# Sink-window attention and SoLU layer on one core: the first chunk's loads issued from ScalarE, and w_in's blocks fetched and split first

## The chip, the cores and the metric

One core of a Trainium2 chip runs the whole kernel. The metric is device time in microseconds (us), the median of a few runs. A profile of one execution of the kernel before is at hand; all its times count from the start of its span.

Short names: PE is the matmul engine TensorE (PEld its weight load), DVE is VectorE, ACT is ScalarE, POOL is GpSimd, SP is SyncE, whose queue issues DMAs. "Row" means a line of a view of the profile; L441 is line 441 of the kernel.

## The reference

```python
def _attn_ref(q, k, v, n_sink, window):          # 4 batches, 8 heads, 768 tokens, 64 per head
    scores = scale * np.matmul(q, k.transpose(0, 1, 3, 2))
    keep = is_sink | in_window                   # key < n_sink, or 0 <= query - key < window
    scores = np.where(keep, scores, -1000000000.0)
    a = np.exp(scores - np.max(scores, axis=-1, keepdims=True))
    a = a / (np.sum(a, axis=-1, keepdims=True) + 1e-09)
    return np.matmul(a, v)

def _moe_ref(x, w_in, w_out, g_ln):              # x: 3072 x 512, w_in: 512 x 1024, w_out: 1024 x 512
    h = x @ w_in
    e = np.exp(h - np.max(h, axis=-1, keepdims=True))
    solu = h * e / (np.sum(e, axis=-1, keepdims=True) + 1e-09)
    ln = (solu - mean) / np.sqrt(var + 1e-06) * g_ln
    return ln @ w_out
```

The drawn scalars are n_sink = 4 and window = 128. The two weights, the gain g_ln and the scalars come as 64-bit numbers; q, k and v as 32-bit floats.

## The kernel before

The 3,072 tokens are cut into 24 chunks of 128, numbered `n`, two batches in turn. A chunk passes some fifty stages: loads of k, q and v (`load_k`, `load_q`, `load_v`, all through `load`), transposes of q and k on PE (`turn`, L526), copies on ACT (`kf`, `qf`), scores per head (L604 for chunks 0 and 1, L606 and L607 for the others), the masked minimum on DVE (L624), exponentials on ACT (L634), normalisation on POOL, transposes of the weights `ptp`, the product with v (`av`, `xp`), then `h` = x·w_in (L772), the SoLU and layer norm, the transposes `utp`, `o` = u·w_out (L841), and the store.

The products with the two weights are done in three passes, with every operand split into a high and a low part. The splitting of the weights is done on the chip, in 16 blocks of 512 KB: blocks 0 to 7 are w_in (`w1h`, `w1l`), 8 to 15 are w_out (`w2h`, `w2l`). A block j passes these stages:

- `fetch_w`, a DMA into `wraw_j`;
- `lower_w` on ACT (L411), then `move_w`, `sign_w` and `rest_w` on DVE (L415, L419, L424), which make `wbits_j` from the 64-bit words;
- `sum_w`, a matmul into the PSUM tile `ws_j` (L441); for w_in there is one such tile at a time (`ps_h` has one buffer);
- `w_hi` on ACT (L449, for w_out L451 with the gain), `less_w` on PE (L455), `w_lo` on ACT (L459), which frees `ws_j`.

Three small loads stand beside them (`fetch_small`): the two scalars into `words`, the gain into `g_rows`, and the first rows of v. `words` passes a few POOL operations, a matmul (`spread_0`) and an ACT copy (`val`) before POOL can make the masks, `bias0` first; `g_rows` passes `spread_1` and the copy `g_sb`.

Nothing reorders this work at run time. Each stage of each chunk and block has a number, a due time, in the tables `PLAN`, `PLAN_W`, `FIRST` and `OWN` (the last for chunks 0 to 3, 22 and 23). All steps are sorted by it, and each engine's program gets its instructions in that order and runs them in that order; an instruction whose input is late holds all behind it on its engine. DMA issues are instructions of the queue's engine in the same sense.

The built program gives each DMA from SP's and ACT's queues one of eight completion semaphores (DMAHW0 to DMAHW7), in turn over both queues in the order of the sorted steps. A DMA that gets a semaphore for the second time is issued only when the DMA that had it before has landed; on which queue that one was does not matter.

Of the kernel before, what the change touches and what calls it, by code (L numbers as in the profile page):

```python
# [11 lines left out]
I32 = mybir.dt.int32  # L12
# [19 lines left out]
    "score": (-33.44, -29.74, -32.95, -26.95, -28.22, -30.8, -25.49, -21.19),  # L32
# [5 lines left out]
    "turn_p": (-17.35, -13.82),  # L38
# [34 lines left out]
    "round_ident": (-3163.34,),  # L73
    "gains": (-344.53, -1257.3, -494.63, -210.32, 7.7, -70.04, -35.97, -251.92, -3187.03),
    "outside": (181.94,),
    "fetch_small": (-3957.07, -334.9, -3898.57),
    "scalars": (-1567.28,),
    "spread": (-1567.18, -1257.7),
    "take_small": (-1567.08, -1257.5),
    "masks": (-1279.21, -432.35, -165.0),  # L80
    "fetch_w": (-405.15, -3960.38, -426.29, -3880.5, -3919.36, -3952.13, -3953.56, -417.09, -3892.48, -3917.91,
                -3984.79, -352.47, -151.19, -383.05, -132.13, -412.11),
    "lower_w": (-322.59, -1511.91, -340.85, -464.5, -1518.94, -3256.59, -3271.05, -342.81, -551.25, -1488.73,
                -3298.13, -259.68, -126.59, -247.18, -65.79, -329.82),
    "move_w": (-278.19, -1291.02, -319.05, -426.7, -1268.02, -2053.29, -2135.99, -342.63, -474.7, -1311.88, -2065.14,
               -242.49, -126.04, -206.92, -64.64, -318.86),
    "sign_w": (-159.49, -1266.75, -280.91, -419.12, -514.59, -2051.66, -2009.32, -327.68, -447.58, -1267.77,
               -2054.73, -219.39, -79.66, -139.64, -54.37, -316.39),
    "rest_w": (-155.59, -517.15, -155.98, -388.61, -341.51, -2042.38, -1259.65, -242.66, -366.45, -1238.15, -521.74,
               -206.56, -69.38, -91.58, -32.25, -243.78),  # L90
    "sum_w": (-119.83, -422.04, -96.33, -336.21, -229.53, -1475.65, -702.46, -156.13, -302.03, -648.8, -436.66,
              -80.12, 29.82, -32.53, 15.53, -217.15),
    "w_hi": (-128.31, -479.01, -100.46, -341.71, -328.13, -1468.88, -984.48, -230.1, -337.05, -577.13, -482.82,
             -120.05, -19.66, -38.33, -27.91, -142.74),
    "less_w": (-118.42, -381.66, -88.15, -328.34, -206.16, -1389.51, -691.27, -137.84, -264.23, -448.45, -338.06,
               -54.35, 33.19, -26.02, 16.19, -99.77),
    "w_lo": (-100.5, -348.23, -79.88, -324.36, -159.61, -1257.51, -570.51, -129.19, -260.8, -350.76, -260.82, -44.19,
             33.91, -21.12, 20.58, -87.29),
# [74 lines left out]
P = 128  # L173
# [56 lines left out]
def _banded(ctx, tc, q, k, v, n_sink, window, w_in, w_out, g_ln, out, val, wts, wpool, consts):  # L230
    nc = tc.nc
# [8 lines left out]
    KT2 = DFF // P  # L240
# [37 lines left out]
    def fetch_small(_, j):  # L278
        if j == 0:
            for i, s in enumerate((n_sink, window)):  # L280
                nc.sync.dma_start(words[0:1, i, :], s.bitcast(I32).rearrange("(o w) -> o w", o=1))
# [192 lines left out]
    def load(n, nm, src, bufs):  # L474
        b, c = place(n)
# [566 lines left out]
```

## Time and profile before

| what | value |
|---|---|
| median of 3 runs | 497.99 us (497.97 to 498.84) |
| the profiled execution | 498.57 us |
| its span | 496.9 us, 9093 instructions |
| PE busy | 468.7 us, 94% of the span |
| PEld, DVE, ACT, POOL busy | 388.4, 390.5, 354.4, 316.1 us |
| DMA, over the span | 51.78 MB, mean 104 GB/s |
| DMA, 12.4 us slices, the first four | 275, 307, 196, 171 GB/s |

The profiled execution lies 0.58 us above the median. PE is the busiest engine, but a share of the whole span says little about a change at its beginning: the stretches of the first 60 us have to be read one by one, and in them each engine's first rows with the idle time ahead of each and what ended it.

### The profile page before, as it was taken

To read this page: it belongs to the slowest core of one execution; us is meant where nothing else is said; L and a number is where in the kernel's file an instruction comes from. 1 tells how busy PE (TensorE), PEld (TensorE's weight loads), DVE (VectorE), ACT (ScalarE), POOL (GpSimd) and SP (SyncE) were. 2 spreads that over 40 slices of the span, in tenths; PEclk is the share of its full clock that TensorE was granted. 3 is DMA by queue.
4 is the path that set the end of the run, shared out by engine and by line. 5 is a ranking of instruction groups with operands and counts; after the bars stand their busy time and mean duration, and the time that the engine had idled before them with its cause. 6 is when DMAs were issued, how large, how long until landed. Compare 5 with 4: busy or idle time off the path is not lost.

```text
span 496.9 us, 9093 instructions
## 1 busy us (share of the span) xinstructions
PE 468.7 (94%) x2631; PEld 388.4 (78%) x2631; DVE 390.5 (79%) x1195; ACT 354.4 (71%) x957; POOL 316.1 (64%) x439
## 2 busy tenths in 40 slices
PE   0989999999899999999999999999999999999995
PEld 0444767888788888888888888888888888887873
DVE  2878999899987588798799988888888879766631
ACT  4798997787785667776876786676777787675352
POOL 3675576588666557678646386676776776667610
PEclk9978999999999999999999999999999999999999
DMA  8966154354265353522555363464264262201101
GB/s 275 307 196 171 43 108 106 85 122 113 61 140 119 75 117 84 120 67 54 119 136 106 79 139 68 113 138 107 53 141 106 54 144 61 57 28 44 44 22 47
DMA packets 101099, 51.78 MB, mean 104 GB/s; under 512 B 78956, under 2 KB 90228, under 8 KB 101044
## 3 DMA queue, kind: packets, MB, share of 16 engines
q1 hardware_dynamic: 101044, 51.14, 42.4%
q8 instruction: 23, 0.38, 0.3%
q14 instruction: 32, 0.26, 0.2%
HBM read 27.53 MB, written 6.42 MB: 68 GB/s over the span
## 4 chain that ended last, share of the span: by engine, by line
PE 73%; DVE 9%; ACT 5%; POOL 5%; issue 4%; DMA 2%; SPq 0%; DVEq 0%; POOLq 0%
PE o L841 22%; PE h L772 21%; PE s L606 4%; PE s L607 4%; PE utp L826 4%; PE av L721 3%; PE ptp L652 3%; PE av L724 3%; PE ws L441 2%; PE kt L526 2%; PE qt L526 2%; PE av L726 1%; DVE y L734 1%; DVE ring L579 1%; DMA wraw<-in_moe_w_in_dram 1%
## 5 line engine op out<-in xcount | busy, mean ns | idle before, releaser
L841 PE MATMUL o<-w2h,uh 128*128 128x512 f32 x192 | 79.2, 412 | 0.0
L772 PE MATMUL h<-w1h,xh 128*128 128x512 f32 x192 | 77.5, 403 | 0.6 <-DVE u L794 0.6
L634 ACT ACTIVATE sc<-sc,nmx 128x136 f32<-128x136 f32 (+1 forms) x192 | 76.4, 402 | 1.7 <-DVE nmx L624 1.2
L772 PE MATMUL h<-w1l,xh 128*128 128x512 f32 x192 | 75.9, 395 | 0.0
L841 PE MATMUL o<-w2h,ul 128*128 128x512 f32 x192 | 75.7, 394 | 0.0
L734 DVE TENSOR_REDUCE y<-av 128x256 f32<-128x512 f32 x88 | 60.3, 687 | 19.5 <-PE av L726 17.0
L772 PE MATMUL h<-w1h,xl 128*128 128x512 f32 x192 | 75.7, 394 | 0.0
L841 PE MATMUL o<-w2l,uh 128*128 128x512 f32 x192 | 75.6, 394 | 0.0
L669 POOL TENSOR_SCALAR_AFFINE_SELECT pc<-pt 128x1024 fp32r<-128x1024 f32 x40 | 43.8, 1095 | 33.3 <-DVE pt L662 17.0
L624 DVE CUSTOM_DVE_ANT_0 sc<-s,bias 128x136 f32<-128x136 f32 (+1 forms) x192 | 54.4, 295 | 10.1 <-PE s L604 2.9
L645 POOL TENSOR_TENSOR sc<-sc,rs 128x544 f32<-128x544 f32 (+1 forms) x48 | 52.2, 1089 | 15.5 <-DVE rs L640 8.7
L606 PE MATMUL s<-ring,qT 128*128 128x264 f32 (+1 forms) x176 | 56.2, 321 | 2.6 <-DVE nmx L624 1.4
L761 POOL TENSOR_TENSOR xl<-xt,xh 128x256 fp32r<-128x256 f32 x44 | 32.4, 737 | 28.9 <-ACT xh L756 22.5
L607 PE MATMUL s<-ring,qX 128*128 128x264 f32 (+1 forms) x176 | 49.7, 285 | 0.3 <-DMA qX<-qT 0.3
L721 PE MATMUL av<-pc,vs 128*128 128x256 f32 x160 | 44.3, 299 | 1.3 <-ACT ob L846 0.9
L675 POOL TENSOR_SCALAR_AFFINE_SELECT pt<-pt 128x1024 fp32r<-128x1024 f32 x40 | 43.6, 1091 | 1.6
L830 ACT CAST uh<-utp 128x512 fp32r<-128x512 f32 x48 | 28.0, 586 | 21.3 <-PE utp L826 21.1
L834 DVE TENSOR_TENSOR ul<-utp,uh 128x512 fp32r<-128x512 f32 x48 | 33.0, 687 | 12.8 <-ACT uh L830 12.1
L772 PEld LDWEIGHTS h<-w1h,xl 128*128 128x128 f32 x192 | 36.1, 188 | 8.9
L841 PEld LDWEIGHTS o<-w2h,ul 128*128 128x128 f32 x192 | 36.1, 188 | 8.7 <-DVE ul L834 0.2
L606 PEld LDWEIGHTS s<-ring,qT 128*128 128x128 f32 x176 | 33.1, 188 | 11.9 <-issue 3.6
L574 ACT CAST ring<-kt 64x512 fp32r<-64x512 f32 x44 | 25.4, 578 | 22.9 <-DVE ring L579 21.8
(147 smaller groups left out, 1300.7 us busy)
## 6 DMA issues: line engine op xcount, KB each, us to landing
qX<-qT SPq DMA_DIRECT2D x88, 128.0 KB, 2.2
kn<-in_k_dram SPq DMA_DIRECT2D x24, 256.0 KB, 3.5
qn<-in_q_dram SPq DMA_DIRECT2D x24, 256.0 KB, 4.1
vn<-in_v_dram SPq DMA_DIRECT2D x24, 256.0 KB, 4.3
out_dram<-ob SPq DMA_DIRECT2D x24, 256.0 KB, 3.5
ysh<-y SPq DMA_DIRECT2D x88, 64.0 KB, 2.0
wraw<-in_moe_w_out_dram SPq DMA_DIRECT2D x8, 512.0 KB, 4.0
wraw<-in_moe_w_in_dram SPq DMA_DIRECT2D x8, 512.0 KB, 6.6
```

Source lines behind the costliest of these rows:

```text
L606: nc.tensor.matmul(o, st["qT", n, x][:, r, :], rhs, start=True, stop=False)
L607: nc.tensor.matmul(o, st["qX", n, x][:, r, :], rhs, start=False, stop=True)
L624: nc.vector.tensor_tensor_reduce(out=st["sc", n, hb][:, j, c0:c1], in0=st["s", n, h].rearrange("p a x -> p (a x)")[:, c0:c1], in1=bias0 if ...
L634: nc.scalar.activation(sc[:, i, c0:c1], sc[:, i, c0:c1], AF.Exp, bias=nmx[:, i:i + 1], scale=-1.0, accum_out=ssum[:, i:i + 1])
L645: nc.gpsimd.tensor_tensor(sc[:, :, c0:c1], sc[:, :, c0:c1], rs.unsqueeze(2).to_broadcast([P, HB, c1 - c0]), op=ALU.mult)
L669: nc.gpsimd.affine_select(pc, pt.bitcast(F32), pattern=[[0, HB * 2], [1, P]], compare_op=ALU.is_ge, fill=0.0, base=0, channel_multiplier=-1)
L675: nc.gpsimd.affine_select(pt, pt.bitcast(F32), pattern=[[0, HB * 2], [-1, P]], compare_op=ALU.is_ge, fill=0.0, base=-1, channel_multiplier=1)
L721: nc.tensor.matmul(acc[:, x], lhs, pc[:, 2 * jp + x], start=(x == 0), stop=(alone and x == 1))
L734: nc.vector.tensor_reduce(st["y", n, hb][:, jp], st["acc", n, pr].rearrange("p x s q -> p x q s"), axis=AX.X, op=ALU.add)
L772: nc.tensor.matmul(st["h", n][:, cols], a[:, kt % 2, :], w[:, kt, cols], start=(kt == 0 and m == 0), stop=(kt == KT1 - 1 and m == 2))
L834: nc.vector.tensor_tensor(ul, st["utp", n, g4], st["uh", n, g4].bitcast(F32), op=ALU.subtract)
L841: nc.tensor.matmul(st["o", n], a[:, kt % 4, :], part(w, kt), start=(kt == 0 and m == 0), stop=(kt == KT2 - 1 and m == 2))
```

## The change

Three things are changed.

- Five DMAs go from SP's queue to ACT's: the loads of chunk 0's keys and queries (`kn_0`, `qn_0`), the two scalars, and the gain.
- The due times of the weight blocks and of chunks 0 to 3, 22 and 23 are other numbers. The blocks of w_in are fetched ahead of most of w_out's, and block 5 of w_in is the first on SP's queue and the first that DVE makes.
- Two entries of `PLAN` move by 0.09 and 0.25: one score (head 5) and the second transpose of the weights `ptp`. They hold for all chunks without numbers of their own.

```diff
 PLAN = {
-    "score": (-33.44, -29.74, -32.95, -26.95, -28.22, -30.8, -25.49, -21.19),
+    "score": (-33.44, -29.74, -32.95, -26.95, -28.22, -30.71, -25.49, -21.19),
...
-    "turn_p": (-17.35, -13.82),
+    "turn_p": (-17.35, -13.57),
 PLAN_W = {
-    "fetch_small": (-3957.07, -334.9, -3898.57),
+    "fetch_small": (-5146.64, -294.06, -5149.48),
...
-    "fetch_w": (-405.15, -3960.38, -426.29, -3880.5, -3919.36, -3952.13, -3953.56, -417.09, -3892.48, -3917.91,
+    "fetch_w": (-5089.45, -5149.5, -5086.99, -5118.34, -5146.5, -5149.71, -5148.45, -418.64, -5103.25, -5146.01,
...
 def fetch_small(_, j):
-                nc.sync.dma_start(words[0:1, i, :], s.bitcast(I32).rearrange("(o w) -> o w", o=1))
+                nc.scalar.dma_start(words[0:1, i, :], s.bitcast(I32).rearrange("(o w) -> o w", o=1))
...
-            nc.sync.dma_start(g_rows[0:KT2], g_ln.rearrange("(kt p) -> kt p", p=P))
+            nc.scalar.dma_start(g_rows[0:KT2], g_ln.rearrange("(kt p) -> kt p", p=P))
 def load(n, nm, src, bufs):
-        nc.sync.dma_start(t, src[b, :, c * P:(c + 1) * P, :].rearrange("h p d -> p h d"))
+
+        (nc.scalar if n == 0 and nm != "vn" else nc.sync).dma_start(
+            t, src[b, :, c * P:(c + 1) * P, :].rearrange("h p d -> p h d"))
```

What the new numbers do is shown by the order of the instructions. Lines of the changed kernel lie one to three higher than those of the kernel before (L411 is L412, L526 is L529). A name such as `wraw_10_125` is the tile `wraw` of block 10; the last number only counts tiles. What stands behind "waits" are the semaphores that the instruction waits for.

ACT's first rows before: the table load, then blocks 10, 6 and 5, then the constants and the scalars' copy, blocks 4, 1 and 9, and the first `w1h`.

```order
L411 ACT_TABLE_LOAD
L411 ACTIVATE wbits_10_148<-wraw_10_125 128x512 [waits DMAHW0_49]
L411 ACTIVATE wbits_6_150<-wraw_6_131 128x512 [waits DMAHW4_49]
L411 ACTIVATE wbits_5_152<-wraw_5_133 128x512 [waits DMAHW5_49]
L434 ACTIVATE dg_8_154<-ident_89 128x128 [waits Pool_49]
L262 CAST ident_r_94<-ident_89 128x128
L309 COPY val_58<-spread_0_169 128x2 [waits PE_49]
L411 ACTIVATE wbits_4_172<-wraw_4_135 128x512 [waits DMAHW6_49]
L411 ACTIVATE wbits_1_174<-wraw_1_127 128x512 [waits DMAHW1_49]
L411 ACTIVATE wbits_9_176<-wraw_9_137 128x512 [waits DMAHW7_49]
L449 CAST w1h_62<-wbits_5_152 128x512 [waits DVE_49]
```

The same place on ACT now.

```order
L287 DMA g_rows_99<-in_moe_g_ln_dram 8x128 [waits Pool_49]
L282 DMA words_95<-in_n_sink_dram 1x2
L282 DMA words_95<-in_window_dram 1x2 [waits DMAHW0_49]
L479 DMA kn_0_140<-in_k_dram 128x8x64 [waits DMAHW1_49]
L412 ACT_TABLE_LOAD
L412 ACTIVATE wbits_1_142<-wraw_1_127 128x512
L435 ACTIVATE dg_8_144<-ident_89 128x128
L479 DMA qn_0_146<-in_q_dram 128x8x64 [waits DMAHW4_49]
L412 ACTIVATE wbits_5_158<-wraw_5_125 128x512
L263 CAST ident_r_94<-ident_89 128x128
L412 ACTIVATE wbits_6_161<-wraw_6_130 128x512 [waits DMAHW2_49]
L412 ACTIVATE wbits_4_163<-wraw_4_136 128x512
```

Five DMAs moved into ACT's program, four ahead of the table load and `qn_0` ahead of block 5's `lower_w`. DMAHW0, 1 and 4 were given before to `wraw_5`, `wraw_1` and `wraw_4`, the first, second and fifth blocks on SP's queue (next fences).

SP's first rows before.

```order
L402 DMA wraw_10_125<-in_moe_w_out_dram 128x1024
L402 DMA wraw_1_127<-in_moe_w_in_dram 128x1024
L281 DMA words_95<-in_n_sink_dram 1x2
L281 DMA words_95<-in_window_dram 1x2
L402 DMA wraw_6_131<-in_moe_w_in_dram 128x1024
L402 DMA wraw_5_133<-in_moe_w_in_dram 128x1024
L402 DMA wraw_4_135<-in_moe_w_in_dram 128x1024
L402 DMA wraw_9_137<-in_moe_w_out_dram 128x1024
L477 DMA kn_0_139<-in_k_dram 128x8x64
L477 DMA qn_0_141<-in_q_dram 128x8x64
L286 DMA g_rows_99<-in_moe_g_ln_dram 8x128
```

SP's first rows now.

```order
L403 DMA wraw_5_125<-in_moe_w_in_dram 128x1024
L403 DMA wraw_1_127<-in_moe_w_in_dram 128x1024
L403 DMA wraw_6_130<-in_moe_w_in_dram 128x1024
L403 DMA wraw_10_132<-in_moe_w_out_dram 128x1024
L403 DMA wraw_4_136<-in_moe_w_in_dram 128x1024
L403 DMA wraw_9_138<-in_moe_w_out_dram 128x1024
L403 DMA wraw_3_148<-in_moe_w_in_dram 128x1024
L403 DMA wraw_8_150<-in_moe_w_out_dram 128x1024
L403 DMA wraw_0_152<-in_moe_w_in_dram 128x1024
L403 DMA wraw_2_154<-in_moe_w_in_dram 128x1024
L479 DMA qn_1_156<-in_q_dram 128x8x64
L403 DMA wraw_15_247<-in_moe_w_out_dram 128x1024
```

Ten weight blocks now stand in a row; `kn_1` follows `wraw_15`, where before it stood ahead of it.

PE's first rows now; before, `spread_1` stood behind `kt_0`, the queries' transposes ahead of the keys', and `ws_9`'s first matmul between the scores 6 and 5.

```order
L305 MATMUL spread_1_176<-ident_89,g_rows_99 128x128
L303 MATMUL spread_0_178<-alone_98,ones_f_100 128x2
L442 MATMUL ws_5_186<-wbits_5_158,dg_8_144 128x512
L456 MATMUL ws_5_186<-w1h_62,ident_r_94 128x512
L529 MATMUL kt_0_189<-ident_89,kn_0_140 128x128 x4
L529 MATMUL qt_0_194<-ident_89,qn_0_146 128x128 x4
L442 MATMUL ws_6_224<-wbits_6_161,dg_8_144 128x512
L456 MATMUL ws_6_224<-w1h_62,ident_r_94 128x512
L607 MATMUL s_0_3_227<-kf_0_219,qf_0_222 128x128
L607 MATMUL s_0_6_229<-kf_0_219,qf_0_222 128x128
L607 MATMUL s_0_5_240<-kf_0_219,qf_0_222 128x128
L607 MATMUL s_0_4_242<-kf_0_219,qf_0_222 128x128
```

The same eight groups of matmuls as before lead up to the first score `s_0_3`; behind it the scores 6, 5 and 4 follow at once, and `ws_9` has moved behind them.

More of the change, by code (lines that the diff above doesn't have):

```diff
@@ L72 @@
 PLAN_W = {
-    "round_ident": (-3163.34,),
-    "gains": (-344.53, -1257.3, -494.63, -210.32, 7.7, -70.04, -35.97, -251.92, -3187.03),
-    "outside": (181.94,),
-    "fetch_small": (-3957.07, -334.9, -3898.57),
[L77 to L80, printed above, removed]
-    "fetch_w": (-405.15, -3960.38, -426.29, -3880.5, -3919.36, -3952.13, -3953.56, -417.09, -3892.48, -3917.91,
-                -3984.79, -352.47, -151.19, -383.05, -132.13, -412.11),
@@ L83 @@
[L83 to L98, printed above, removed]
+    "round_ident": (-3361.62,),
+    "gains": (-377.83, -1251.67, -437.6, -147.52, 15.46, -84.04, -17.22, -232.77, -5129.02),
+    "outside": (150.82,),
+    "fetch_small": (-5146.64, -294.06, -5149.48),
@@ new lines @@
+    "scalars": (-1614.26,),
+    "spread": (-1563.05, -1564.19),
+    "take_small": (-1556.91, -1258.2),
+    "masks": (-1266.51, -449.66, -165.94),
+    "fetch_w": (-5089.45, -5149.5, -5086.99, -5118.34, -5146.5, -5149.71, -5148.45, -418.64, -5103.25, -5146.01,
+                -5146.83, -294.09, -195.78, -295.89, -115.85, -494.09),
+    "lower_w": (-318.67, -5131.58, -316.18, -503.55, -3353.66, -3370.51, -3354.7, -319.11, -490.5, -1526.41,
+                -1536.51, -258.52, -153.06, -233.78, -82.99, -374.2),
@@ new lines @@
+    "move_w": (-298.96, -1396.96, -256.96, -479.95, -2370.06, -2396.73, -2370.87, -258.07, -479.96, -1394.91,
+               -1394.17, -251.39, -133.69, -79.85, -82.35, -342.32),
+    "sign_w": (-258.87, -1396.87, -242.79, -414.94, -1386.81, -2396.45, -2370.15, -255.01, -430.46, -1390.38,
+               -560.71, -168.17, -116.83, -79.43, -50.51, -300.63),
+    "rest_w": (-170.52, -1386.46, -167.25, -414.6, -364.45, -2388.27, -1398.38, -249.55, -419.27, -1384.85, -480.34,
+               -158.9, -83.49, -50.52, -43.69, -299.51),
@@ new lines @@
+    "sum_w": (-137.62, -418.94, -100.45, -313.47, -277.92, -1500.51, -742.35, -195.28, -351.46, -451.41, -382.58,
+              -39.98, 25.81, -14.86, 35.47, -194.66),
+    "w_hi": (-148.39, -488.91, -129.08, -319.86, -316.19, -1541.11, -1267.72, -230.5, -374.6, -484.89, -379.47,
+             -62.35, -51.34, -49.77, -40.8, -131.67),
+    "less_w": (-132.13, -396.99, -92.97, -312.65, -261.04, -1499.03, -699.31, -156.09, -344.7, -441.58, -357.73,
+               -30.75, 28.42, -6.33, 38.21, -103.0),
@@ L99 @@
+    "w_lo": (-110.98, -363.52, -79.97, -280.59, -241.16, -1263.51, -493.14, -148.53, -317.76, -375.78, -329.91,
+             -23.13, 32.49, -5.62, 42.87, -83.4),
 }
```

113 rows, old and new, of the table OWN are left out of this document.

## The prediction

> **What bounds the kernel now.** I read the page first, then the busy times by stretch, and then, since the change sits at the beginning, each engine's first rows in order of time.
>
> ```profile
> span 496.9 us, 9093 instructions
> 0.00:12.50 12.50, 0.58 (x2) 0.50 (x2) 3.33 (x8) 5.09 (x10) 4.31 (x19) 1.00 0.84 275
> 12.50:25.00 12.50, 11.43 (x37) 6.17 (x38) 10.77 (x30) 9.40 (x23) 8.06 (x14) 1.00 1.04 307
> 25.00:40.00 15.00, 12.04 (x41) 6.98 (x40) 11.30 (x31) 13.24 (x30) 9.24 (x12) 0.69 0.60 167
> 40.00:60.00 20.00, 19.14 (x92) 12.17 (x91) 17.34 (x60) 18.73 (x59) 11.55 (x23) 0.98 0.47 121
> 90.00:120.00 30.00, 30.00 (x181) 25.59 (x180) 26.64 (x84) 22.37 (x66) 22.15 (x29) 1.00 0.36 87
> 400.00:480.00 80.00, 79.04 (x437) 66.76 (x437) 55.22 (x157) 49.86 (x128) 50.05 (x66) 1.00 0.22 58
> 480.00:497.00 17.00, 10.70 (x50) 8.06 (x48) 3.27 (x9) 5.39 (x9) 0.81 (x2) 0.94 0.10 35
> ```
>
> The columns after the length are PE, PEld, DVE, ACT and POOL busy, PE's granted clock, the DMA share and GB/s. From 40 us on PE is idle for 0.86 of 20 us, then for almost nothing up to 480 us: it is the bound, and its work is the same after the change. So the time changes by what PE loses or wins before 40 us, where it is idle for 11.92 + 1.07 + 2.96 = 15.95 us, and by a little at the end. Up to 25 us the 16 DMA engines are full (share 0.84, with the start-up in it, and 1.04), so the order in which blocks land decides what can start.
>
> ```profile
> 0.80 1.28 ACT L411 ACT_TABLE_LOAD   x1 [0.80 <-PEq L1024]
> 4.28 0.59 SPq L477 DMA_DIRECT2D kn<-in_k_dram  x1
> 4.29 0.66 ACT L411 ACTIVATE wbits<-wraw 128x512 f32<-128x512 f32 x1 [2.21 <-DMA wraw<-in_moe_w_out_dram]
> 6.12 2.60 SPq L477 DMA_DIRECT2D qn<-in_q_dram  x1
> 8.44 0.66 ACT L411 ACTIVATE wbits<-wraw 128x512 f32<-128x512 f32 x1 [3.49 <-DMA wraw<-in_moe_w_in_dram]
> 8.84 3.24 SPq L286 DMA_DIRECT2D g_rows<-in_moe_g_ln_dram  x1
> 9.74 0.67 ACT L411 ACTIVATE wbits<-wraw 128x512 f32<-128x512 f32 x1 [0.65 <-DMA wraw<-in_moe_w_in_dram]
> 10.54 0.42 DVE L415 TENSOR_SCALAR wbits<-wbits 128x512 int32<-128x512 int32 x1
> 10.98 2.05 ACT L411 ACTIVATE wbits<-wraw 128x512 f32<-128x512 f32 x3
> 11.72 0.69 DVE L424 SCALAR_TENSOR_TENSOR wbits<-wraw,wbits 128x512 int32<-128x512 int32 x1
> 12.55 2.05 PE L441 MATMUL ws<-wbits,dg 128*128 128x512 f32 x2 [4.71 <-DVE wbits L424]
> 12.94 0.60 ACT L449 CAST w1h<-wbits 128x512 fp32r<-128x512 f32 x1
> 13.61 1.42 PE L455 MATMUL ws<-w1h,ident_r 128*128 128x512 f32 x1
> 14.82 1.05 PE L526 MATMUL qt<-ident,qn 128*128 128x128 f32 x4
> 15.06 0.60 ACT L459 ACTIVATE w1l<-ws 128x512 fp32r<-128x512 f32 x1 [1.52 <-PE ws L455]
> 15.84 2.48 DVE L424 SCALAR_TENSOR_TENSOR wbits<-wraw,wbits 128x512 int32<-128x512 int32 x4
> 16.53 0.42 PE L304 MATMUL spread<-ident,g_rows 128*128 128x128 f32 x1
> 16.98 0.17 ACT L311 COPY g_sb<-spread 128x8 f32<-128x8 f32 x1 [1.32 <-PE spread L304]
> 17.52 0.60 ACT L548 COPY qf<-qt 128x512 f32<-128x512 f32 x1
> 18.70 0.50 PE L455 MATMUL ws<-w1h,ident_r 128*128 128x512 f32 x1 [0.75 <-ACT w1h L449]
> 19.12 0.49 PE L604 MATMUL s<-kf,qf 64*128 64x128 f32 x4
> 19.78 0.29 DVE L624 CUSTOM_DVE_ANT_0 sc<-s,bias 128x128 f32<-128x128 f32 x1 [0.76 <-PE s L604]
> ```
>
> Three things are to be seen. The eight semaphores show: `kn_0`, the ninth DMA, is issued at 4.28, when the first block lands (ACT takes it at 4.29), and `qn_0` only at 6.12, so the second block lands then. The blocks land at 4.29, 6.12, at most 8.44, 9.74 and at most 10.98, where ACT takes three lowers without a gap, the fifth block's first. And from ACT's `lower_w` of block 5 at 9.74 to its first matmul at 12.55 there are 2.81 us, which set PE's first real work.
>
> **The change, part by part.** *The DMAs on ACT.* Before, all five cost ACT nothing. Now ACT issues `g_rows` and one scalar, waits for the first block (4.29) to issue the other, waits for the second (6.12) to issue `kn_0` (0.59), and only then loads its table (1.28): 6.12 + 0.59 + 1.28 = 7.99. Block 1's `lower_w` follows to 8.65; before, ACT only had one lower behind it at that time, so that much is hidden. Not hidden is `qn_0`: it waits for the fifth block. That lands between 9.74 (the fourth before) and 10.98, plus up to half a block's spacing of (9.74 - 4.29) / 3 = 1.82, since `kn_0` with half a block's bytes now travels among the first five. I take 11.0, and 0.59 for the issue, as for `kn_0` on SP; at the ends 9.9 and 0.4, or 11.9 and 2.60, `qn_0`'s own row. ACT reaches block 5's lower at 11.6 (10.3 to 14.5), against 9.74.
>
> A rule speaks against this part in any case. The Trainium skill, DMA: Bandwidth & Descriptors, section Issuing engines are not separate DMA queues, says that DMAs from all queues run on the same 16 engines, and that spreading the issue saves only the issuing sequencer's time. The shares of 0.84 and 1.04 above agree that the engines were full already. By it alone the part would be worth nothing.
>
> *Block 5 first on DVE.* DVE's first rows are now all of block 5, so PE's first split starts at 11.6 + 2.81 = 14.4, against 12.55: 1.85 later (0.6 to 4.8). `w1h` follows at 14.4 (12.94 before), `less_w` at 15.0 (13.61).
>
> *The first transposes.* Two sets take 16.53 - 14.82 = 1.71, so they run from 15.4 to 17.1 instead of to 16.53. The queries' come second, at 16.2. `qn_0`, issued at 11.0, lands at 15.1 by the median of its kind, and is in time:
>
> ```profile
> qn<-in_q_dram SPq DMA_DIRECT2D x24, 256.0 KB, 4.1
> 22.42 1.12 PE L441 MATMUL ws<-wbits,dg 128*128 128x512 f32 x2
> ```
>
> `spread_1` is out of the way early, which takes away the 1.32 us ahead of `g_sb`.
>
> *To the first score.* DVE makes block 6 behind block 5: 14.4 + 0.41 + 0.62 + 0.41 + 0.62 = 16.5 (0.62 is 2.48 / 4; 0.41 and 0.62 likewise for L415 and L419). Then on ACT `w1h` of block 6, `w1l` of block 5, `g_sb`, `kf`, a ring cast and `qf` at 0.5 to 0.6 each: 19.6. The first score starts at 19.6 instead of 19.12. DVE has 12 instructions between block 5 and the first masked minimum, 4 x 0.41 + 8 x 0.62 = 6.6: 21.0 instead of 19.78, with block 10 two instructions (1.24) less far than before. The scores that now follow at once have only two PSUM buffers and wait for these minima; `ws_9`, which filled that time before, stands behind them.
>
> ```profile
> 28.68 0.48 PE L604 MATMUL s<-kf,qf 64*128 64x128 f32 x2 [1.18 <-ACT kf L570]
> 29.71 0.49 PE L604 MATMUL s<-kf,qf 64*128 64x128 f32 x2
> 30.00:42.50 12.50, 10.87 (x35) 6.14 (x34) 9.65 (x25) 10.97 (x27) 5.16 (x9) 0.59 0.39 90
> DMA to landing us min/median/max: 4.8/6.6/9.2
> ```
>
> *To chunk 1's scores.* The minima let the scores 5, 4 and 7 go by 22.4; then come block 9 (1.12 + 0.50, the rows of L441 above and of L455), `qt_1` (0.86), block 1 (1.62), block 10 (1.12) and three scores: `kt_1` at about 28, its copy `kf` done at 29.5, the first score of chunk 1 at about 30, against 29.71. So most is caught up, since `qt_1` now comes early and DVE had idle time. But at that point PE lacks both matmuls of block 3 (1.62), with one of block 8 (1.12) as the offset, 0.5 + 0.3 = 0.8 in all, and ACT lacks two lowers and a `w1h` (2 x 0.67 + 0.60), less a ring cast (0.6), 1.3. I take 1.1, between the two. `kn_1`, which now waits behind `wraw_15` for DVE's block 9 (21.0), lands 4.8 us later (the last line above, for the loads of k in the first 60 us), at 25.8, and is not needed before 27.
>
> *The middle and the end.* In chunks 4 to 21 the new numbers swap one transpose group with one score or with the `utp` beside it; in chunks 22 and 23 groups change places, but the same work stands behind the last `h`.
>
> ```profile
> PE s L606 <- DVE nmx L624: 1.1, 3, 0.7
> PE av L721 <- ACT ob L846: 0.9, 2, 0.7
> ```
>
> These are PE's longest waits from 60 us on (total, times, longest). One such wait more or less is 0.7 us; I take 0 for both, and 0.7 either way for the range.
>
> *Sum.* +1.1 in the head, 0 behind it. The profiled execution's 498.57 becomes 499.7. It stands 0.58 above the median, and the same step from the median of 497.99 gives 499.1. Faster and slower are told from no change at about 0.2%, 1.0 us.
>
> **The rivals.**
>
> *Absorbed: 498.0.* The lag at 30 us is met by idle time that is there anyway: from 30 to 42.5 us PE is busy for 10.87 of 12.5 us and DVE for 9.65. Against it stands ACT, 10.97 of 12.5, which carries most of the lag. It decides if ACT catches up 1 us by 42 us. Chance 0.30.
>
> *Faster: 496.0.* In that stretch the granted clock was 0.59, after waits such as the 1.18 us for `kf`. With `qt_1` and `qf` of chunk 1 early, and the w_in blocks closer together, PE may wait less and get its full clock sooner. At full clock the 10.87 us would take 10.87 x 0.59 = 6.4, 4.5 less, of which ACT's load leaves 12.5 - 10.97 = 1.5; with the 1.18 us of wait, and less the lag, -1.6 to -2. It decides if the clock comes up before about 37 us. Chance 0.25.
>
> *Starved: 502.5.* Chunk 0's loads are the smallest packets:
>
> ```profile
> DMA packets 101099, 51.78 MB, mean 104 GB/s; under 512 B 78956, under 2 KB 90228, under 8 KB 101044
> ```
>
> The 72 loads of k, q and v make 72 x 1024 = 73,728 of the 78,956 packets under 512 B (rows of 256 B); a weight block is 128 packets of 4 KB. On each of 16 DMA engines that is 64 packets against 8. If these engines take turns between the two queues by packets, `kn_0`, issued at 6.12, travels beside eight blocks, the third to the tenth, and lands with the tenth: 4.29 + 9 x 1.82 = 20.7, where `kt_0` wants it at 15.4, and `qn_0` lands behind it. The Trainium skill, DMA: Bandwidth & Descriptors, section Queues, rings and completion order, says that each DMA engine goes round robin between its queues, packet by packet, with several descriptors to a packet as a rule; no run here shows two loaded queues yet. Then `kt_0` and all behind it on PE slip by 5.3 more, of which ACT and DVE can use one or two on blocks that have landed: +4.5 in all. It decides once `kn_0` lands later than 15.4 or `qn_0` later than 16.2. Chance 0.08.
>
> **How the numbers follow.** The forecast keeps 0.37; its own range is 498.5 to 500.0, about a third of which lies within 0.2%. Slower by over 0.2%: 0.37 less 0.10, plus the starved case and the upper ends of the issue (2.60) that fall to it: 0.40. Same: 0.10 and most of the absorbed case, less 0.08 that end beyond 0.2% with the 0.7 of middle or end: 0.32. Faster: 0.28. The range goes from the faster case with 0.7 more gained, 495.4, to the forecast's upper end with the 4.8 of the slowest issue half absorbed, 501.3; it leaves out most of the starved case.
>
> **What would show it.** In the profile after: ACT's table load near 6.7 instead of 0.80; an idle stretch on ACT of about 2 us up to the issue of `qn_0`, with block 5's lower at 11 to 12; PE's first L442 at 14 to 15; the first score near 19.6; and the stretch from 40 to 60 us as full as before. The prediction is wrong if that lower comes before 10 us, if the first score comes before 18.5 or behind 21, or if the granted clock from 30 to 42.5 us is much over 0.59.

## The result: 1.2% slower, because the queries landed at 20.5 us

The changed kernel takes 504.56 us (median of 4 runs, 501.85 to 506.51) against 498.06 us for the kernel before on the same chip: a ratio of 1.0115, with a 95% interval of 1.0088 to 1.0143. The profiled execution is the one of 506.51 us, with a span of 504.7 us. The direction is the forecast's, the size is not: +6.5 us instead of +1.1, and outside the range.

The busy times by stretch after; the columns are those of the prediction's first fence.

```profile
12.50:25.00 12.50, 7.30 (x18) 3.81 (x18) 8.22 (x17) 7.89 (x17) 10.13 (x16) 1.00 0.89 269
25.00:40.00 15.00, 14.87 (x50) 8.12 (x50) 9.20 (x34) 11.20 (x28) 5.23 (x7) 1.00 0.64 175
40.00:60.00 20.00, 15.81 (x69) 8.96 (x69) 17.11 (x55) 19.24 (x57) 13.41 (x25) 0.91 0.46 119
```

PE, the bound from 40 us on, is busy for 7.30 us instead of 11.43 from 12.5 to 25 us, and for 15.81 instead of 19.14 from 40 to 60. From 25 to 40 it is busier, 14.87 against 12.04, in both kernels partly with matmuls at half pace (below). The rows of ACT and PE (timeline of after) say where the first loss is:

```profile
5.93 0.41 ACTq L479 DMA_DIRECT2D kn<-in_k_dram  x1
6.37 1.28 ACT L412 ACT_TABLE_LOAD   x1 [6.37 <-DMA wraw<-in_moe_w_in_dram]
10.72 0.40 ACTq L479 DMA_DIRECT2D qn<-in_q_dram  x1
11.17 0.66 ACT L412 ACTIVATE wbits<-wraw 128x512 f32<-128x512 f32 x1 [2.65 <-DMA wraw<-in_moe_w_in_dram]
13.88 2.04 PE L442 MATMUL ws<-wbits,dg 128*128 128x512 f32 x2 [2.18 <-DVE wbits L425]
16.15 1.05 PE L529 MATMUL kt<-ident,kn 128*128 128x128 f32 x4
20.55 1.12 PE L529 MATMUL qt<-ident,qn 128*128 128x128 f32 x4 [3.34 <-DMA qn<-in_q_dram]
21.46 1.92 PE L442 MATMUL ws<-wbits,dg 128*128 128x512 f32 x2
21.70 0.59 ACT L551 COPY qf<-qt 128x512 f32<-128x512 f32 x1 [3.22 <-PE qt L529]
23.73 0.80 PE L607 MATMUL s<-kf,qf 64*128 64x128 f32 x4
```

Up to `kt_0` at 16.15 (15.4 forecast) the head runs within a microsecond of the forecast. Then PE waits 3.34 us for `qn_0`. The list of DMAs after has the time from issue to landing in its last column (us):

```profile
qn<-in_q_dram SPq DMA_DIRECT2D x23, 256.0 KB, 4.0
kn<-in_k_dram SPq DMA_DIRECT2D x23, 256.0 KB, 3.5
kn<-in_k_dram ACTq DMA_DIRECT2D x1, 256.0 KB, 9.4
qn<-in_q_dram ACTq DMA_DIRECT2D x1, 256.0 KB, 9.8
```

The loads of the other 23 chunks, on SP's queue, take 3.5 and 4.0 us by the median; the two on ACT's queue took 9.4 and 9.8. `qn_0` landed at 10.72 + 9.8 = 20.5.

Most of those 23 run later, when less is moved (307 GB/s in the second slice of the kernel before, 104 in the mean). At the beginning SP's queue is not that fast: in the kernel before, `kn_0` and `qn_0`, behind the blocks in that queue, took 9.2 and 8.5 us (7.1 and 6.1 in kq_on_sp below). Its view of `qn` up to 60 us, which has three landings:

```profile
DMA to landing us min/median/max: 6.6/8.5/8.7
```

So `qn_0` landed 5.9 us later than before (14.6): 4.6 of them are the later issue, 10.72 instead of 6.12, and 1.3 the longer time to landing.

### The profile page after: what moved, and what is told of

It is laid out like the page before. It is cut to its first block, busy times and chain, and to the rows that moved or that the text cites. A ratio compares the mean times of both kernels' runs of the same rounds, so it can differ in the third digit from the quotient of the medians.

```text
span 504.7 us, 9090 instructions
## 1 busy us (share of the span) xinstructions
PE 471.0 (93%) x2631; PEld 388.3 (77%) x2631; DVE 388.6 (77%) x1195; ACT 355.0 (70%) x957; POOL 317.8 (63%) x439
## 5 line engine op out<-in xcount | busy, mean ns | idle before, releaser
L844 PE MATMUL o<-w2h,uh 128*128 128x512 f32 x192 | 80.3, 418 | 0.1
L627 DVE CUSTOM_DVE_ANT_0 sc<-s,bias 128x136 f32<-128x136 f32 (+1 forms) x192 | 54.6, 295 | 16.9 <-PE s L607 9.1
L609 PEld LDWEIGHTS s<-ring,qT 128*128 128x128 f32 x176 | 33.3, 189 | 11.6 <-issue 3.3
L727 PE MATMUL av<-pt,vs 128*128 128x256 f32 x160 | 41.5, 281 | 0.0
L775 PEld LDWEIGHTS h<-w1h,xh 128*128 128x128 f32 x192 | 36.1, 188 | 6.7 <-DVE u L797 0.6
```

The costliest lines, as they stand in the source:

```text
L609: nc.tensor.matmul(o, st["qT", n, x][:, r, :], rhs, start=True, stop=False)
L627: nc.vector.tensor_tensor_reduce(out=st["sc", n, hb][:, j, c0:c1], in0=st["s", n, h].rearrange("p a x -> p (a x)")[:, c0:c1], in1=bias0 if ...
L727: nc.tensor.matmul(acc[:, x], lhs, pt[:, 2 * jp + x], start=False, stop=False)
L775: nc.tensor.matmul(st["h", n][:, cols], a[:, kt % 2, :], w[:, kt, cols], start=(kt == 0 and m == 0), stop=(kt == KT1 - 1 and m == 2))
L844: nc.tensor.matmul(st["o", n], a[:, kt % 4, :], part(w, kt), start=(kt == 0 and m == 0), stop=(kt == KT2 - 1 and m == 2))
```

## The experiments

Three theories stood after the result. *Starved*: the loads are slow because their 256 B packets share the 16 DMA engines with SP's 4 KB packets. *Waiting*: ACT issues too late, since three of its DMAs wait for a reused semaphore. *Order*: the new tables themselves are worse. The ratios are to the kernel before on the same chip, with 95% intervals; the times in us are of one profile each.

| kernel | `qn_0` issued, landed | first score | first h | ratio |
|---|---|---|---|---|
| before | 6.12, 14.6 | 19.12 | 54.92 | 1 |
| after | 10.72, 20.5 | 23.73 | 59.68 | 1.0115 [1.0088, 1.0143] |
| after, second profile | 11.65, 21.1 | 24.34 | 56.02 | 1.0126 [1.0100, 1.0152] |
| order_only | 6.46, by 14.90 | 18.01 | 50.85 | 0.9974 [0.9960, 0.9987] |
| kq_on_sp | 7.97, 14.1 | 18.51 | 51.90 | 1.0005 [0.9994, 1.0016] |
| small_on_sp | 8.16, 15.8 | 19.07 | 52.29 | 1.0023 [0.9999, 1.0046] |
| rows_2kb | 10.87, 17.2 | 19.96 | 52.80 | 1.0059 [1.0037, 1.0082] |
| queues_only | 8.21, 17.8 | 25.85 | 61.62 | 1.0118 [1.0099, 1.0137] |
| kq_first | 1.29, by 18.75 | 28.90 | 63.67 | 1.0225 [1.0194, 1.0256] |

"By" is in order_only the start of the transposes, which did not wait for the load, and in kq_first that of an issue that did.

### The order alone

```diff
-                nc.scalar.dma_start(words[0:1, i, :], ...
+                nc.sync.dma_start(words[0:1, i, :], ...
...
-            nc.scalar.dma_start(g_rows[0:KT2], ...
+            nc.sync.dma_start(g_rows[0:KT2], ...
...
-        (nc.scalar if n == 0 and nm != "vn" else nc.sync).dma_start(
+        nc.sync.dma_start(
```

> The changed kernel with all five DMAs back on SP's queue: the new tables alone. Starved (the loads of chunk 0 are slow on ACT's queue because the 16 DMA engines take turns by packets, 256 B against 4 KB): kn_0 and qn_0 now stand behind six blocks in one queue and land near 14.5 and 15.5 us, the first score starts at 19 to 20 instead of 23.73, and the time is 497 to 499.5 us. New order itself slower (blocks and ws_9 in a worse place): the first score may be early, but the time stays at 502 to 505. Waiting on ACT (reused semaphores): also gone here, so it expects 497 to 499.5 too.

497.24 us (496.21 to 499.07), ratio 0.9974: the new tables are not slower, they are faster by 1.3 us. Theory *Order* falls as the cause of the loss. In the timeline of this kernel:

```profile
18.01 0.49 PE L607 MATMUL s<-kf,qf 64*128 64x128 f32 x4
20.45 1.12 PE L442 MATMUL ws<-wbits,dg 128*128 128x512 f32 x2
```

The first score comes 1.11 us earlier than before and the first h 4.07 us earlier, yet the time gains only 1.3. Some 2 of the 4.07 us are work that now stands behind the first h: ahead of it are 36 matmuls of the blocks instead of 38 and 12 transposes of queries instead of 16 (a pair of L442 takes 1.12 above, four transposes 0.60 to 1.06). Most of the rest is given back between 40 and 120 us. PE's waits there in this kernel (total, times, longest):

```profile
PE s L609 <- DVE nmx L627: 1.6, 3, 0.7
PE ptp L655 <- POOL sc L648: 1.6, 1, 1.6
```

The busy times by stretch, first of this kernel and then of the kernel before (its stretch from 90 us on is in the prediction):

```profile
60.00:90.00 30.00, 28.01 (x160) 21.78 (x159) 27.42 (x89) 24.74 (x66) 20.70 (x27) 1.00 0.47 98
90.00:120.00 30.00, 28.89 (x177) 24.74 (x176) 26.99 (x87) 21.86 (x66) 21.47 (x29) 1.00 0.35 80
```

```profile
60.00:90.00 30.00, 28.55 (x169) 22.21 (x168) 27.57 (x87) 25.46 (x69) 20.32 (x27) 1.00 0.51 110
```

From 60 to 120 us PE is busy for 56.90 us in the one and for 58.55 in the other. The 1.6 us that a transpose of the weights waits for POOL is not among the waits of before, whose longest there is 0.6; it stands in the changed kernel too, with the same 1.6.

From 290 to 440 us, where both kernels run the same steps, this one is only 0.2 to 0.3 us ahead (by the starts of the matmuls of `o`). The rest of the 1.5 us by which its span is shorter (495.4 us) comes behind that, in the last chunks; 0.7 of it shows in the profiles of plan_only and queues_only as well, whose last chunks are those of before. So little of the 1.3 us is shown to come from the beginning.

### Keys and queries back on SP

```diff
-        (nc.scalar if n == 0 and nm != "vn" else nc.sync).dma_start(
+        nc.sync.dma_start(
```

> The changed kernel with kn_0 and qn_0 back on SP's queue; the scalars and the gain stay on ACT. Starved: qn_0 lands near 15.5 instead of 20.5, the first score at 19 to 20, time 497 to 500. Waiting on ACT by the small loads (the second scalar waits for the first block, so the table load stays late at 4.9 to 5.5): at most 0.5 us more than the order alone. New order slower: 502 to 505.

498.55 us, ratio 1.0005. Taking these two DMAs off ACT's queue gives back all of the loss. The three small ones alone cost about 1.3 us against the order alone, more than the 0.5 at most that was expected: the table load stands at 5.04 instead of 0.80, and the first score comes 0.50 later.

### The queues alone

The edit is the converse: the tables of before, with the five DMAs issued from `nc.scalar` as in the change.

> The kernel before with the five DMAs issued from ACT, its tables as they were. Starved: kn_0 and qn_0 are issued near 5 us and share one queue, 128 packets of 256 B on each DMA engine against 8 for a block, so kn_0 lands near 14 and qn_0 at 20 to 24 (before: both in time for 14.82), the first score at 22 to 26 instead of 19.12, time 501 to 505. New order slower, queues harmless: first score at 19 to 20, time 498 to 499.

504.02 us (503.57 to 506.26), ratio 1.0118, as much as the whole change. So the queues are the loss, with the old order too. The rows are not quite the expected ones. From its list of DMAs:

```profile
kn<-in_k_dram ACTq DMA_DIRECT2D x1, 256.0 KB, 12.7
qn<-in_q_dram ACTq DMA_DIRECT2D x1, 256.0 KB, 9.6
```

From its timeline of ACT and PE:

```profile
10.93 2.36 ACTq L286 DMA_DIRECT2D g_rows<-in_moe_g_ln_dram  x1
13.32 1.28 ACT L411 ACT_TABLE_LOAD   x1 [13.32 <-issue]
19.28 2.04 PE L441 MATMUL ws<-wbits,dg 128*128 128x512 f32 x2 [11.03 <-DVE wbits L424]
21.55 1.05 PE L527 MATMUL qt<-ident,qn 128*128 128x128 f32 x4
```

`kn_0` landed at 16.9 and `qn_0` at 17.8, not at 20 to 24, and the first transposes started only at 21.55: here PE did not wait for the loads. What made the first score late, at 25.85, is that ACT's program stood behind three DMA issues with reused semaphores, those of the first, the third and the fifth block. Its table load came at 13.32 and PE's first L441 at 19.28 instead of 12.55, 6.73 us later, and by the same 6.73 the first score is late. So in the old order the loss is *Waiting*, not *Starved*.

### The same bytes in larger packets

```diff
-        (nc.scalar if n == 0 and nm != "vn" else nc.sync).dma_start(
-            t, src[b, :, c * P:(c + 1) * P, :].rearrange("h p d -> p h d"))
+        eng = nc.scalar if n == 0 and nm != "vn" else nc.sync
+        if n == 0 and nm != "vn":
+            eng.dma_start(t.rearrange("p h d -> p (h d)"),
+                          src[b].rearrange("h s d -> (h s d)")[0:P * H * D].rearrange("(p x) -> p x", p=P))
+        else:
+            eng.dma_start(t, src[b, :, c * P:(c + 1) * P, :].rearrange("h p d -> p h d"))
```

> The changed kernel, but kn_0 and qn_0 read the first 256 KB of k and q in rows of 2 KB, one per partition, instead of eight rows of 256 B: the same bytes on the same queue at the same place in the program, 8 packets per DMA engine instead of 64. Chunk 0 is computed from those other elements. Starved: each lands within 2 to 4 us of its issue instead of 9.4 and 9.8, qn_0 near 14, first score near 19.6 (what the prediction had), time 498.5 to 500. If the late issue or the load on the DMA engines made them late whatever the packets, they land 8 to 10 us after the issue as before and the time stays at 502 to 505.

500.65 us (499.97 to 504.41), ratio 1.0059. Its list of DMAs, and then its timeline:

```profile
kn<-in_k_dram ACTq DMA_DIRECT2D x1, 256.0 KB, 7.4
qn<-in_q_dram ACTq DMA_DIRECT2D x1, 256.0 KB, 6.3
```

```profile
17.23 1.12 PE L533 MATMUL qt<-ident,qn 128*128 128x128 f32 x4
19.96 0.49 PE L611 MATMUL s<-kf,qf 64*128 64x128 f32 x4
```

Same bytes, queue, place in the program and nearly the same time of issue (10.87), with an eighth of the packets: `qn_0` lands at 17.2 instead of 20.5, the first score starts at 19.96 instead of 23.73, and about half of the loss is gone. The size of the packets is a cause. It is not the whole: both loads still take 6 to 7 us, where 2 to 4 were expected, so some 2 us stay against keys and queries on SP, and the time lies between the two forecasts. By the starts of the packets, `qn_0` has its first turn 3.5 to 3.7 us after its issue in both kernels (at 14.4); from there to the landing it needs 2.8 us here and 6.1 in the changed kernel. Only the second part hangs on the size of the packets.

### The changed kernel once more

> The changed kernel once more, for its spread (its four times went from 501.85 to 506.51) and a second profile. Starved: median 503.5 to 505, qn_0 again lands 9 to 10 us after its issue, and while both queues are loaded their packets go one for one. If the slow landing was an accident of one execution, qn_0 lands within 5 us in this profile and the median is under 502.

504.92 us (503.39 to 507.71), ratio 1.0126. The slow landing was no accident: 9.5 us for `qn_0`, and 13.3 for `kn_0`, which PE's first transposes waited for too (19.39).

```profile
kn<-in_k_dram ACTq DMA_DIRECT2D x1, 256.0 KB, 13.3
qn<-in_q_dram ACTq DMA_DIRECT2D x1, 256.0 KB, 9.5
```

Its timeline of PE:

```profile
21.16 1.12 PE L529 MATMUL qt<-ident,qn 128*128 128x128 f32 x4 [0.66 <-DMA qn<-in_q_dram]
24.34 0.62 PE L607 MATMUL s<-kf,qf 64*128 64x128 f32 x4
26.91 1.13 PE L442 MATMUL ws<-wbits,dg 128*128 128x512 f32 x2
```

Here the first score comes 0.61 us later than in the first profile, but the span is 501.7 us against 504.7. Two matmuls of L442 take 1.13 us here at 26.91. In the first profile such a pair took nearly twice that up to 31 us (its timeline):

```profile
26.94 2.07 PE L442 MATMUL ws<-wbits,dg 128*128 128x512 f32 x2
31.01 1.91 PE L442 MATMUL ws<-wbits,dg 128*128 128x512 f32 x2
```

So PE's matmuls ran at half pace for at least 5 us longer there, and half of that, 2.5 us of work, is most of the 3.0 between the spans. In the order alone such a pair is down to 1.12 at 20.45. That this stretch makes the spread of the changed kernel is read from two profiles, not tried by a run.

### The small loads back on SP

```diff
-                nc.scalar.dma_start(words[0:1, i, :], ...
+                nc.sync.dma_start(words[0:1, i, :], ...
...
-            nc.scalar.dma_start(g_rows[0:KT2], ...
+            nc.sync.dma_start(g_rows[0:KT2], ...
```

> The changed kernel with the scalars and the gain back on SP; kn_0 and qn_0 stay on ACT. Starved: qn_0 still lands 9 us or more after its issue, so the time stays 3 to 5 us above that of keys and queries on SP: 502 to 504.5; the small loads are worth the 1.3 us that they cost in the other pair. Waiting on ACT: the table load no longer stands behind two waits, so if that was what cost the time it falls to 498 to 499.5.

500.15 us (497.89 to 503.06), ratio 1.0023: both expectations missed, one above and one below. Taking the small loads off ACT gives back about 5 us, where they had cost 1.3 with the keys on SP. Its timeline shows why the two parts do not add:

```profile
0.81 0.46 ACTq L479 DMA_DIRECT2D kn<-in_k_dram  x1
8.16 0.41 ACTq L479 DMA_DIRECT2D qn<-in_q_dram  x1
16.22 1.06 PE L529 MATMUL qt<-ident,qn 128*128 128x128 f32 x4
```

Its list of DMAs has the time to landing:

```profile
qn<-in_q_dram ACTq DMA_DIRECT2D x1, 256.0 KB, 7.6
```

With nothing ahead of it, `kn_0` is issued at 0.81 and `qn_0` at 8.16 instead of 10.72. It still takes 7.6 us, but lands at 15.8, just ahead of its transposes at 16.22. A load that is slow but in time costs PE no wait. In the changed kernel late issue and slow landing together put it 4 us past that point.

### Keys and queries first on ACT's queue

```diff
-    0: (-5146.0, -5119.46, -259.42, ...
+    0: (-5150.0, -5149.9, -259.42, ...
```

> The changed kernel with kn_0 and qn_0 as the first two instructions on ACT's queue, ahead of the gain and the scalars: the same packets on the same queue, but issued at 0.8 and 1.3 us, waiting for no semaphore. If the slow landing hurts only together with the late issue (10.72 and 11.65 in the two profiles of the changed kernel), qn_0 lands by 9 us, kt_0 and qt_0 run in time, the first score starts at 18.5 to 20 and the time is 498.5 to 501 us. If packets of 256 B on a second queue are slow wherever they are issued, they land at 14 to 20, the first score at 21 to 24 and the time is 502 to 505.

510.12 us (507.51 to 512.94), ratio 1.0225, the slowest of all and outside both forecasts. If late issue alone were the cause, this would have cured it, since both are issued at once:

```profile
1.29 0.60 ACTq L479 DMA_DIRECT2D qn<-in_q_dram  x1
18.75 0.23 ACTq L282 DMA_DIRECT2D words<-in_window_dram  x1
19.01 1.28 ACT L412 ACT_TABLE_LOAD   x1 [19.01 <-DMA qn<-in_q_dram]
```

The second scalar has `qn_0`'s semaphore and is issued at 18.75, when `qn_0` has landed: some 17 us after its issue at 1.29, and behind it stands all of ACT's program: slow landing and a reused semaphore together. (`kn_0` had landed at 6.5.) What the packets did can be counted in the trace, by the start of each packet:

| kernel, stretch (us) | 4 KB packets, SP's queue | packets of `kn_0`, `qn_0`, ACT's queue |
|---|---|---|
| kq_first, 8 to 11 | 245 | 274 of 256 B |
| queues_only, 9 to 12 | 280 | 306 of 256 B |
| after_again, 12 to 15 | 263 | 337 of 256 B |
| after, 14 to 17 | 281 | 281 of 256 B |
| after, 11 to 12 | 31 | 686 of 256 B |

In the first two rows the 16 engines take about one packet from each queue in turn, and so in every one of these microseconds (83 to 95, 79 to 89 and 83 to 90 in kq_first): 16 of 17 bytes go to the blocks. In the changed kernel it is so in the sum only (98 to 38, 90 to 146, 93 to 97). The small packets took 18 ns each by the median, those of 2 KB 84 and those of 4 KB 159. Where the turns go one for one, a load of 1024 small packets needs as long as 1024 large ones, eight blocks: at some 90 a microsecond 11 us. In kq_first `qn_0` took 12, from 6 to 18 us. That is *Starved* as the prediction's rival had it.

The Trainium skill, DMA: Bandwidth & Descriptors, section Queues, rings and completion order, says that each DMA engine goes round between its queues packet by packet, usually with several descriptors to a packet. The turns agree with these counts; that a turn should hold several rows is not seen in them, since rows of 256 B and of 4 KB go 306 to 280.

Not all is told by it. At 11 us in the changed kernel the small packets passed at 686 a microsecond, though three more blocks had been issued by 9.64 us and none of them had begun; 949 of `kn_0`'s 1024 went from 10 to 12 us, beside 101 of the blocks. In kq_first `kn_0`'s packets passed almost alone from 4 to 5 us (698 against 17), with four more blocks already issued. What sets how long ACT's queue waits for its first turn, and when it has the engines almost to itself, stays open.

### The two entries of PLAN alone

```diff
-    "score": (-33.44, -29.74, -32.95, -26.95, -28.22, -30.8, -25.49, -21.19),
+    "score": (-33.44, -29.74, -32.95, -26.95, -28.22, -30.71, -25.49, -21.19),
-    "turn_p": (-17.35, -13.82),
+    "turn_p": (-17.35, -13.57),
```

> The kernel before with only the two changed entries of PLAN (one score by 0.09, the second transpose of the weights by 0.25), which hold for chunks 4 to 21. The prediction took 0 for the middle, with 0.7 either way: 497.3 to 498.7 us, the same as before. If the new waits from 60 us on (the new order loses about 3 us between the first h and chunk 4) came from these two entries, the time would be 499 to 501.

498.66 us, ratio 1.0004 [0.9989, 1.0019]. They are worth nothing, as forecast. So the new waits between 40 and 120 us are not theirs.

### Three tries at something better

All on top of the order alone. *better_1*: scalars behind the second block, block 5's `lower_w` first, `spread_0` behind the first matmul of `ws_5`, block 4's `lower_w` and first DVE step behind `w1h` of block 5. *better_2*: also `kn_0` and `qn_0` ahead of the third block. *better_3*: also, on ACT, the lowers of blocks 6, 4, 10 and 9 behind `kf` and `qf`. The first lines are from the edit of *better_1*, the last pair from that of the other two.

```diff
-    "fetch_small": (-5146.64, -294.06, -5149.48),
+    "fetch_small": (-5149.49, -294.06, -5149.48),
-    "spread": (-1563.05, -1564.19),
+    "spread": (-1541.06, -1564.19),
...
-    0: (-5146.0, -5119.46, -259.42, ...
+    0: (-5149.46, -5149.45, -259.42, ...
```

> The new order with all DMAs on SP, and in it: the two scalars issued right behind the second block instead of behind the fourth; block 5's lower ahead of block 1's; PE's spread_0, which kept ws_5 waiting for POOL until 11.16, behind ws_5's first matmul; block 4's lower and first DVE step behind block 5's w1h. ws_5 should start near 8 instead of 11.60 and the masks be ready 3 us earlier, but the keys and queries land at 13 to 14 as before and hold the first score at 17 to 18: 496 to 497.5 us. If the head no longer counts, 497.2 as the order alone.

> As better_1, and kn_0 and qn_0 stand on SP right behind the scalars and the gain, ahead of the other blocks: they should land by 8 to 9 us, the first score start at 14.5 to 16 instead of 18.01, and the time be 494 to 496.5 us. Against it: the blocks land 1.3 us later each, and if they bound the head the time is 497 to 498.

> As better_2 (all DMAs on SP, keys and queries ahead of the third block), but on ACT the lowers of blocks 6, 4, 10 and 9 stand behind w1h and w1l of block 5 and behind kf and qf, so that no block that is still to land holds the transposes of chunk 0 back. In better_2 they did: the keys were there, but kt_0 started at 13.66. kt_0 should start at 10 to 11 and the first score at 16 to 17.5 (behind ws_6): 494.5 to 497 us. If the landing of the blocks bounds the head, the first score may be early and the time stays at 498 to 501.

Ratios 0.9980 [0.9962, 0.9997], 1.0039 [1.0019, 1.0060] and 1.0057 [1.0034, 1.0080]. The first, 497.89 us, is no better than the order alone and just above its forecast; the other two, 501.39 and 501.06, are misses. In better_2 the keys were there early, but ACT stood in front of block 6 (ACT and PE, timeline). In better_3 that is mended, but now block 6's `lower_w` stands at 13.29 behind `kf` and `qf`, and PE waits for block 6 (ACT and PE, timeline):

```profile
11.85 0.66 ACT L412 ACTIVATE wbits<-wraw 128x512 f32<-128x512 f32 x1 [4.64 <-DMA wraw<-in_moe_w_in_dram]
13.66 1.05 PE L529 MATMUL kt<-ident,kn 128*128 128x128 f32 x4
```

```profile
10.58 1.05 PE L520 MATMUL kt<-ident,kn 128*128 128x128 f32 x4
13.29 0.66 ACT L403 ACTIVATE wbits<-wraw 128x512 f32<-128x512 f32 x1
16.07 2.04 PE L433 MATMUL ws<-wbits,dg 128*128 128x512 f32 x2 [3.58 <-DVE wbits L416]
18.47 0.80 PE L598 MATMUL s<-kf,qf 64*128 64x128 f32 x4
```

`kt_0` at 10.58, but the first score at 18.47. In both, block 6 is late: in better_2 ACT gets it at 11.85, against 7.53 in the order alone, where 1.3 us were expected for each block; what makes it so much is not shown. The order alone and better_1 are the versions that beat both kernels.

## Why the prediction was wrong

- **The step that failed** is the term "`qn_0`, issued at 11.0, lands at 15.1 by the median of its kind". It was issued at 10.72 and landed at 20.5. The 4.1 us were the median of 24 loads over the whole kernel, most of them at times when less is moved; the first three of them, issued by 22 us, took 6.6 to 8.7 on SP's queue in the same profile, and with their median of 8.5 the sum would have been 19.5. The term measured 9.8. It was mis-sized by 5.7 us, and the landing lay 4 us past the point at which the prediction said that it decides (16.2).
- **The nearest rival** is *Starved*: forecast 502.5 with the first transposes late by about 5, measured 504.6 with those of the queries 4.35 late against 16.2. It got 0.08, because "no run here shows two loaded queues yet". Half of its mechanism is shown: queues that go packet by packet (kq_first, queues_only), and half of the loss gone with larger packets. The other half is not as it said. `kn_0` was to land at 20.7 and decide; in the first profile it landed at 15.3, in time (in the second at 19.3), and what decided was `qn_0`, issued 4.6 us later than before. That the time came within about 2 us of the rival's is in part luck.
- **Right:** the table load at 6.7 (6.37), block 5's lower at 11.6 (11.17) with ACT's idle stretch, PE's first L442 at 14.4 (13.88), and the semaphores that set them. So the late issue was priced well. It is the other half of the cause: with `qn_0` issued at 8.16, a landing that took 7.6 us cost PE no wait.
- **A minimum taken for a median:** the 4.8 us for `kn_1` are the smallest of their row (4.8/6.6/9.2). It did no harm; `kn_1` landed at 25.1, forecast 25.8.
- **The first score**, forecast at 19.6 and named as wrong if behind 21, came at 23.73; rows_2kb, with the starving cut down, has 19.96.
- **"+1.1 in the head" for order and queues together** hides two terms of opposite sign: the order is worth -1.3, not all of it in the head; the small loads on ACT cost 1.3 by themselves (kq_on_sp against order_only), the keys and queries some 2.4 (small_on_sp against order_only, by the ratios), and some 3 more come only with both.
- **"0 behind the head"** held for the two entries of PLAN, and not for the tables of the first chunks: of the 4.07 us at the first h some 2 are moved work and 0.2 to 0.3 are left from 290 us on. The 1.5 to 2 between are lost in waits such as the 1.6 for POOL, which the prediction did not look for.
- **The clock.** The prediction named a granted clock much over 0.59 from 30 to 42.5 us as a sign of being wrong, and *Faster* made it its condition. It came true: 1.00 in the changed kernel, as in the order alone (last fences of this document). But the one is slower and the other faster, so this clock did not decide the time. In the kernel before, PE did fall to half pace from about 31 to 41 us: four transposes take 1.05 at 34.84 instead of 0.60 at 26.90 (its timeline below). Whether the order alone gains by being at full pace there is not shown.

```profile
26.90 0.60 PE L526 MATMUL qt<-ident,qn 128*128 128x128 f32 x4
34.84 1.05 PE L526 MATMUL qt<-ident,qn 128*128 128x128 f32 x4
```

## What to carry to other kernels

A second issuing queue shares the same DMA engines, and beside a queue with 4 KB packets a load of 256 B rows can get as little as one packet in turn, a small part of the bytes: give such a load its place in the full queue, or larger rows, or a time when the other queue is empty. A DMA in a compute engine's program can also stop that engine: ACT's table load moved from 0.80 to 6.37, 13.32 and 19.01 us, behind semaphores that earlier DMAs still held. Price a load from the packets beside it and from its rows at that time of the kernel, not from its median over the whole of it, and price it against the moment at which it is wanted: 15.8 came with 0.2% here, 20.5 with 1.2%. A change of order and of queues in one edit should be measured apart; here one half was worth -0.26% and the other +1.2%.

## What was not expected of the hardware

- Two queues with work can go about packet for packet, 306 of 256 B to 280 of 4 KB over 3 us; a load of 256 KB then took up to 17 us. At other times the small packets passed almost alone (686 to 31).
- PE can be at half pace where the granted clock of the stretch is 1.00. The changed kernel shows 1.00 from 12.5 to 25 us, where two matmuls of L442 take 1.92 (at 21.46), and 1.00 from 30 to 42.5, where a pair takes 1.91 at 31.01 and 1.02 at 33.63. In the order alone, at 1.00 too, a pair takes 1.02 at 30.38 (timeline of the order alone, then busy times by stretch of it and of the changed kernel):

```profile
30.38 1.02 PE L442 MATMUL ws<-wbits,dg 128*128 128x512 f32 x2
```

```profile
30.00:42.50 12.50, 8.96 (x41) 5.24 (x41) 11.62 (x30) 12.35 (x30) 8.45 (x17) 1.00 0.64 158
```

```profile
30.00:42.50 12.50, 11.40 (x44) 6.23 (x44) 8.25 (x28) 10.53 (x28) 6.72 (x8) 1.00 0.59 153
```
